# Attention forward and backward: six of eight blocks of E transposed on TensorE instead of seven, and the fp32 transposes of X spread over four steps

## The chip, the cores and the metric

One core of one Trainium2 chip runs the whole program in one launch. The metric is the device time in microseconds of one execution; a kernel's time is the median of several runs. A core has five engines with queues of their own: TensorE (PE; its weight loads are shown as PEld), VectorE (DVE), ScalarE (ACT), GpSimd (POOL) and SyncE (SP), which here only issues DMAs. Results of TensorE land in PSUM, in banks of 2 KB a partition; the DMA engines move data between DRAM and SBUF and can transpose blocks of 128 x 128 bf16 on the way. Engines wait for each other by semaphores.

## The reference

The kernel computes the output of a gated attention block and the gradients of all its inputs and weights. With 2048 tokens, width 512 and 32 heads of 16 columns:

```python
def _A_ref(x, wqkv, wo):
    qkv = (x @ wqkv).reshape(B, S, 3, H, Dh).transpose(2, 0, 3, 1, 4)
    q, k, v = qkv[0], qkv[1], qkv[2]
    p = softmax(einsum("bhqd,bhkd->bhqk", q, k) * Dh ** -0.5)
    o = einsum("bhqk,bhkd->bhqd", p, v)
    return o.transpose(0, 2, 1, 3).reshape(B, S, D) @ wo

def _B_ref(x, w1, b1, w2, b2):
    return gelu(layernorm(x) @ w1 + b1) @ w2 + b2

def _fwd_reference(...):
    xn = layernorm(x)
    return x + _A_ref(xn, wqkv, wo) * silu(_B_ref(xn, w1, b1, w2, b2))

_out, _vjp = jax.vjp(_f, A_x, A_wqkv, A_wo, B_w1, B_b1, B_w2, B_b2)
return (_out, *_vjp(grad_out))
```

## The kernel before

The program has three stages. The first computes projections and the gate and leaves operands for attention in DRAM. The second, `attention_core`, is the one that is changed; it lies between about 222 and 1882 us of the span. The third makes the gradients of the weights and of x.

Attention works on pairs of heads (`p`, 16 of them) and chunks of 512 queries (`qc`, four a pair), which makes 64 *blocks*. A block has 16 *steps*, one for each chunk of 128 keys, so the loop runs through 1024 steps `g` and then 20 more that only drain. Scores stand with keys on the partitions. One step handles both heads of the pair (`hj`), so it has an E (the exponentials of the scores) of 128 keys x 2 heads x 512 queries, and a G (E times the gradient that comes in, less a row term) of the same size.

The order within a step is written out by hand at the end of `attention_core`, and each engine runs its part in this order:

- TensorE multiplies out `d` of head 0 for step g (L1105), the scores `s` of both heads for step g+1 (L1083), and `d` of head 1. `s` has one PSUM buffer, `d` three.
- ACT makes E of step g+1 with one exponential (L1092), into a slot of the ring `ets`, which has three slots of four steps each.
- TensorE transposes E of step g-1 (L1167). E has eight blocks of 128 x 128 in a step: four groups of queries x two heads. Seven are transposed here, into the one PSUM buffer `tT`; the eighth is left to the DMA. Which block is left out alternates with every group of four steps, so that the blocks left out of two neighbouring groups lie side by side in `ets`.
- TensorE adds E and G of step g-1, times values and keys, to X (L1197, L1200, L1204), a sum over the block in one PSUM buffer. Then it does a share of Z, the gradients of keys and values (L1281), for the step 20 steps back, from transposed E (`ek`, `ekd`) and transposed G (`gk`).
- VectorE makes G as two products `gts`, one for each head (L1122). Between the two it copies up to two of the seven transposed blocks of step g-1 from `tT` to `ek` (L1179); the table `VCOPY` says how many in which step. After the last step of a block it copies X to SBUF as `xs` (L1213). Two times a block it adds Z to `acc` (L1293, L1295).
- ACT copies the rest of `tT` to `ek` (L1179).
- SyncE issues DMA transposes: in every odd step the two steps' G as a whole (`gk`, L1138, 16 blocks), and every eight steps the blocks of E that were left out (`ekd`): in one DMA of eight blocks where the two groups' slots are neighbours (L1154), otherwise in two of four (L1148, L1152).

In the third step of a block (`FIN_AT = 2`, counted from 0) the X of the block before is finished: TensorE transposes `xs` in four fp32 transposes into `XT`, one of the three buffers of `d` (L1223), VectorE copies it to `xt` (L1235) and takes a reciprocal (L1245), and GpSimd makes the weights W for Z, the attention output and the gradient of the queries.

Of the kernel before, what the change touches and what calls it, by code (L numbers as in the profile page):

```python
# [8 lines left out]
bf16 = mybir.dt.bfloat16  # L9
f32 = mybir.dt.float32  # L10
ACT = mybir.ActivationFunctionType
ALU = mybir.AluOpType
# [1006 lines left out]
def attention_core(ctx, ctx_r, tc, k, grads, Oall, dQall, dKVT_out, ident_f32, ident_bf, npairs=16, nqc=4):  # L1019
# [35 lines left out]
    NB = len(blocks)  # L1055
    NSTEP = NB * 16
    st_s, st_d, st_et, st_gt, st_T = {}, {}, {}, {}, {}
    blk = [dict(Gk={}, Ek={}) for _ in range(NB)]
    cur = {}

    def a_unit(g):
        return (g // 16, g % 16) if 0 <= g < NSTEP else None
# [43 lines left out]
                         start=True, stop=True, tile_position=(r, 0))  # L1106


    VCOPY = (0, 0, 0, 0, 1, 1, 1, 2, 1, 2, 0, 0, 1, 1, 1, 0)

    def emit_mult(g):
        a = a_unit(g)
        if a is None:
            emit_cT(g - 1, 7 - VCOPY[(g - 1) % 16], 7, nc.vector.tensor_copy)
            return
        kb = a[1]
        if kb % 2 == 0:
            cur["gts"] = gtp.tile([128, 2, 2, 512], bf16, name="gts")
        gts = cur["gts"]
        st_gt[g] = gts  # L1120
        for hj in range(2):
            nc.vector.tensor_tensor(out=gts[:, kb % 2, hj, :].rearrange("k (b q) -> k b q", b=4),  # L1122
                                    in0=st_d.pop((g, hj))[:].rearrange("k (b q) -> k b q", b=4),
                                    in1=st_et[g][:, :, hj, kb % 4, :], op=ALU.mult)
            if hj == 0:
                emit_cT(g - 1, 7 - VCOPY[(g - 1) % 16], 7, nc.vector.tensor_copy)

    def emit_dmat(g):
        a = a_unit(g)
        if a is None:  # L1130
            return
        j, kb = a
        kc = kb // 4
        if kb % 4 == 1:
            blk[j]["Gk"][kc] = gbp.tile([128, 4, 2, 4, 128], bf16, name="gk")
        if kb % 2 == 1:
            gk = blk[j]["Gk"][kc][:, kb % 4 - 1:kb % 4 + 1]
            nc.sync.dma_start_transpose(out=gk.rearrange("q r h b k -> q (r h b) k"), in_=st_gt[g][:].rearrange("k a h q -> k (a h q)"))  # L1138


        sl = g // 4 % 3
        if kb % 8 == 4:
            ek = ekd.tile([128, 2, 4, 128], bf16, name="ekd")
            blk[j]["Ek"][(kc - 1, 3)] = ek[:, 0]
            blk[j]["Ek"][(kc, 3)] = ek[:, 1]
            blk[j]["ekd"] = ek
            if sl == 0:
                nc.sync.dma_start_transpose(out=ek[:, 0], in_=ets[:, 2, 3, 1].rearrange("k a q -> k (a q)"))  # L1148
        if kb % 8 == 6:
            ek = blk[j].pop("ekd")  # L1150
            if sl == 0:
                nc.sync.dma_start_transpose(out=ek[:, 1], in_=ets[:, sl, 0, 0].rearrange("k a q -> k (a q)"))  # L1152
            else:
                nc.sync.dma_start_transpose(out=ek[:].rearrange("q c a k -> q (c a) k"),  # L1154
                                            in_=ets[:].rearrange("k s b h a q -> k (s b h) (a q)")[:, 8 * sl - 1:8 * sl + 1]
                                            .rearrange("k x q -> k (x q)"))

    def emit_T(g):
        a = a_unit(g)
        if a is None:  # L1160
            return
        kk = a[1] % 4
        et = st_et[g]
        t = ps_t.tile([128, 7, 128], bf16, name="tT")
        for i in range(7):
            b = i + a[1] // 4 % 2
            nc.tensor.transpose(t[:, i, :], et[:, b // 2, b % 2, kk, :], ident_bf[:])  # L1167
        st_T[g] = t
        if kk == 0:
            cur["ek"] = ekc.tile([128, 4, 7, 128], bf16, name="ek")  # L1170
            blk[a[0]]["Ek"][a[1] // 4] = cur["ek"]

    def emit_cT(g, lo, hi, copy):

        a = a_unit(g)
        if a is None or lo == hi:
            return
        j, kb = a
        copy(out=blk[j]["Ek"][kb // 4][:, kb % 4, lo:hi].rearrange("q i k -> q (i k)").bitcast(f32),  # L1179
             in_=st_T[g][:, lo:hi].rearrange("q i k -> q (i k)").bitcast(f32))  # L1180

    def emit_x(g, part):
        a = a_unit(g)
# [23 lines left out]
    def emit_xs(g):  # L1207
        a = a_unit(g)
        if a is None or a[1] != 15:
            return  # L1210
        j = a[0]
        xs = xsp.tile([128, 512], f32, name="xs", tag="xs")
        nc.vector.tensor_copy(out=xs[:], in_=blk[j].pop("X")[:])  # L1213
        blk[j]["xs"] = xs

    def emit_XT(g):
        j = g // 16 - 1
        if g % 16 != FIN_AT or not 0 <= j < NB:
            return
        xs = blk[j].pop("xs")  # L1220
        XT = ps_d.tile([128, 4, 128], f32, name="XT", tag="d")
        for qb in range(4):
            nc.tensor.transpose(XT[:, qb, :], xs[:, qb * 128:(qb + 1) * 128], ident_f32[:])  # L1223
        blk[j]["XT"] = XT

    def emit_fin(g):
        j = g // 16 - 1
        if g % 16 != FIN_AT or not 0 <= j < NB:
            return
        p, qc = blocks[j]  # L1230
        NQq = k.op0["NATQq"]
        NQd = k.op0["NATQd"]
        XT = blk[j].pop("XT")
        xt = xsp.tile([128, 4, 128], f32, name="xt", tag="xs")
        nc.vector.tensor_copy(out=xt[:], in_=XT[:])  # L1235
        xf = xt[:].rearrange("q b c -> q (b c)")
        XE = xf[:, 0:256].rearrange("q (b h c) -> q b h c", b=4, h=2)
        XG = xf[:, 256:512].rearrange("q (b h c) -> q b h c", b=4, h=2)
        W1, W2 = WT[j % 2]
        st0 = qc * 4  # L1240
        nqs = NQq[:, st0:st0 + 4, :, :]
        ndo = NQd[:, st0:st0 + 4, :, :]
        bc = lambda ap: ap.to_broadcast([128, 4, 2, 16])
        rL = finp.tile([128, 4, 2, 1], f32, name="rL")
        nc.vector.reciprocal(out=rL[:], in_=XG[:, :, :, 17:18])  # L1245
        nc.gpsimd.tensor_tensor(out=W2[:, :, :, 16:32], in0=nqs, in1=bc(rL[:]), op=ALU.mult)  # L1246
        ndl = finp.tile([128, 4, 2, 1], f32, name="ndl")
        nc.gpsimd.tensor_tensor(out=ndl[:], in0=XG[:, :, :, 0:1], in1=rL[:], op=ALU.mult)
        ndr = finp.tile([128, 4, 2, 1], f32, name="ndr")
        nc.gpsimd.tensor_tensor(out=ndr[:], in0=ndl[:], in1=rL[:], op=ALU.mult)  # L1250
        nc.gpsimd.tensor_tensor(out=W1[:, :, :, 0:16], in0=ndo, in1=bc(rL[:]), op=ALU.mult)
        nc.gpsimd.tensor_tensor(out=W1[:, :, :, 16:32], in0=nqs, in1=bc(ndr[:]), op=ALU.mult)
        Ov = Oall[:, st0:st0 + 4, p * 32:(p + 1) * 32].rearrange("q b (h c) -> q b h c", h=2)
        nc.gpsimd.tensor_tensor(out=Ov, in0=XE[:, :, :, 16:32], in1=bc(rL[:]), op=ALU.mult)
        t1 = finp.tile([128, 4, 2, 16], f32, name="t1")
        nc.gpsimd.tensor_tensor(out=t1[:], in0=XE[:, :, :, 0:16], in1=bc(ndl[:]), op=ALU.mult)
        nc.gpsimd.tensor_tensor(out=t1[:], in0=XG[:, :, :, 1:17], in1=t1[:], op=ALU.add)
        rL4 = finp.tile([128, 4, 2, 1], f32, name="rL4")
        nc.gpsimd.tensor_scalar(out=rL4[:], in0=rL[:], scalar1=0.25, scalar2=None, op0=ALU.mult)
        dQv = dQall[:, st0:st0 + 4, p * 32:(p + 1) * 32].rearrange("q b (h c) -> q b h c", h=2)  # L1260
        nc.gpsimd.tensor_tensor(out=dQv, in0=t1[:], in1=bc(rL4[:]), op=ALU.mult)

    def emit_z(g):
        u = z_unit(g)
        if u is None:
            return
        j, kp, qb, part = u
        if part == 0 and qb == 0:
            blk[j]["Z"] = ps_z.tile([128, 512], f32, name="Z", tag="z")
        Z = blk[j]["Z"]  # L1270
        for par in range(2):
            kc = 2 * kp + par
            for hj in range(2):
                r = 64 * par + 32 * hj
                if part == 0:
                    mv = blk[j]["Gk"][kc][:, :, hj, qb, :]
                elif 2 * qb + hj == 7 * (1 - par):
                    mv = blk[j]["Ek"][(kc, 3)]
                else:
                    mv = blk[j]["Ek"][kc][:, :, 2 * qb + hj - par, :]  # L1280
                nc.tensor.matmul(Z[r:r + 32, :], lhsT=WT[j % 2][1 - part][:, qb, hj, :], rhs=mv,  # L1281
                                 start=(part == 0 and qb == 0), stop=(part == 1 and qb == 3), tile_position=(0, r))

# [17 lines left out]
            for b in range(2):  # L1301
                nc.gpsimd.dma_start(out=dv[:, kp, b, :], in_=ob[b * 64:(b + 1) * 64, :])

    FIN_AT = 2
    ZOFF = -20
    late = []
    for hj in range(2):
# [2 lines left out]
    for g in range(NSTEP - ZOFF):  # L1310
# [32 lines left out]
        emit_acc(g + ZOFF)  # L1343
        if g >= NSTEP:
            grads.tail_mid(g - NSTEP)
        emit_cT(g - 1, 0, 7 - VCOPY[(g - 1) % 16], nc.scalar.copy)
        st_T.pop(g - 1, None)
        emit_dmat(g)
        st_gt.pop(g - 2, None)
# [117 lines left out]
```

## Time and profile before

| | us |
|---|---|
| runs before (three) | 2231.56, 2234.59, 2238.38; median 2234.59 |
| profiled execution, its own time | 2229.55 |
| its span, first to last instruction | 2227.8 |
| attention, 222 to 1882 us of the span: TensorE busy | 1640.0 of 1660 |
| VectorE busy there | 1548.7 |
| ScalarE busy there | 1448.6 |
| GpSimd busy there | 423.3 |
| mean granted TensorE clock | 0.993 |

The groups of instructions of the attention loop, as the profile gives them (line, engine, operation, out<-in, shapes, count | busy us, mean ns of one | idle us of the engine just before them and what ended most of it):

```profile
L1122 DVE TENSOR_TENSOR gts<-d,ets 128x512 bf16<-128x512 f32 x2048 | 1363.0, 684 | 99.5 <-ACT ek L1179 20.3
L1092 ACT ACTIVATE ets<-s 128x1024 bf16<-128x1024 f32 x1024 | 1048.7, 1024 | 196.9 <-PE s L1083 94.6
L1167 PE MATMUL tT<-ident_bf,ets 128*128 128x128 bf16 x7168 | 569.2, 219 | 15.9 <-ACT ek L1179 6.1
L1179 ACT COPY ek<-tT 128x448 f32<-128x448 f32 (+2 forms) x1024 | 501.6, 490 | 7.3 <-DVE ek L1179 6.1
L1179 DVE COPY ek<-tT 128x64 f32<-128x64 f32 (+1 forms) x576 | 132.4, 230 | 4.8 <-DMA DSO_s<-gd 3.5
```

A matmul record runs until its last result is out, and the next begins long before: seven transposes of 219 ns each start within half a microsecond. Sums of means of TensorE are therefore more than the time they take. One block of 128 x 128 bf16 is 64 fp32 columns wide in the copies of `tT`, so 448 columns are seven blocks. In all, `q1`, the queue of SyncE's DMAs, moves 424.67 MB; over the attention the DMA engines move 199 GB/s.

### The profile page before, as it was taken

To read this page: it belongs to the slowest core of one execution; us is meant where nothing else is said; L and a number is where in the kernel's file an instruction comes from. 1 tells how busy PE (TensorE), PEld (TensorE's weight loads), DVE (VectorE), ACT (ScalarE), POOL (GpSimd) and SP (SyncE) were. 2 spreads that over 40 slices of the span, in tenths; PEclk is the share of its full clock that TensorE was granted. 3 is DMA by queue.
4 is the path that set the end of the run, shared out by engine and by line. 5 is a ranking of instruction groups with operands and counts; after the bars stand their busy time and mean duration, and the time that the engine had idled before them with its cause. 6 is when DMAs were issued, how large, how long until landed. Compare 5 with 4: busy or idle time off the path is not lost.

```text
span 2227.8 us, 74213 instructions
## 1 busy us (share of the span) xinstructions
PE 2158.9 (97%) x30690; PEld 1204.8 (54%) x30690; DVE 1912.6 (86%) x3626; ACT 1734.3 (78%) x2481; POOL 607.5 (27%) x1387
## 2 busy tenths in 40 slices
PE   6999899999999999999999999999999999899998
PEld 3444455555555555555555555555555555344444
DVE  6676799999999999999999999999999998698624
ACT  5664888888888888888888888888888886584214
POOL 4276413222222222222312222222213223310002
PEclk9999999999999999999999999999999999999999
DMA  7785999999999999999999999999999999899874
GB/s 230 245 275 197 190 200 192 199 203 194 202 201 196 201 192 210 196 204 196 202 201 198 200 194 204 197 195 204 199 201 200 196 213 230 233 251 252 231 202 155
DMA packets 1421747, 461.15 MB, mean 207 GB/s; under 512 B 1334622, under 2 KB 1405662, under 8 KB 1421408
## 3 DMA queue, kind: packets, MB, share of 16 engines
q1 hardware_dynamic: 1406880, 424.67, 100.3%
q0 software_dynamic: 12944, 30.16, 5.2%
q8 instruction: 240, 3.93, 0.8%
q10 hardware_dynamic: 1584, 1.57, 0.2%
q14 instruction: 99, 0.81, 0.1%
HBM read 62.79 MB, written 64.75 MB: 57 GB/s over the span
## 4 chain that ended last, share of the span: by engine, by line
PE 89%; DVE 3%; DMA 3%; ACT 3%; issue 2%; SPq 1%; POOL 1%; DVEq 0%; ACTq 0%; POOLq 0%
PE tT L1167 24%; PE d L1105 14%; PE X L1197 10%; PE Z L1281 10%; PE X L1200 5%; PE X L1204 5%; PE s L1083 2%; PE ps_dw L729 2%; PE ps_dy L902 2%; PE ps_m L367 2%; PE ps_h L352 2%; PE ps_dw L974 2%; PE ps_dh L868 2%; PE XT L1223 1%; PE ps_qkv L210 1%
## 5 line engine op out<-in xcount | busy, mean ns | idle before, releaser
L1122 DVE TENSOR_TENSOR gts<-d,ets 128x512 bf16<-128x512 f32 x2048 | 1363.0, 684 | 99.5 <-ACT ek L1179 20.3
L1092 ACT ACTIVATE ets<-s 128x1024 bf16<-128x1024 f32 x1024 | 1048.7, 1024 | 196.9 <-PE s L1083 94.6
L1167 PE MATMUL tT<-ident_bf,ets 128*128 128x128 bf16 x7168 | 569.2, 219 | 15.9 <-ACT ek L1179 6.1
L1167 PEld LDWEIGHTS <-ets 128*128 128x128 bf16 x7168 | 445.7, 97 | 241.2 <-issue 239.3
L1179 ACT COPY ek<-tT 128x448 f32<-128x448 f32 (+2 forms) x1024 | 501.6, 490 | 7.3 <-DVE ek L1179 6.1
L1105 PE MATMUL d<-QDT,KVT 32*128 32x512 bf16 x2048 | 457.4, 385 | 0.0
L1083 PE MATMUL s<-QDT,KVT 32*128 32x512 bf16 x2048 | 401.3, 380 | 3.0 <-ACT ets L1092 2.7
L1105 PEld LDWEIGHTS <-KVT 32*128 32x128 bf16 x2048 | 145.2, 91 | 323.7 <-issue 323.7
L1197 PE MATMUL X<-ets,NAT 128*32 128x256 bf16 x4096 | 300.5, 284 | 0.1
L1204 PE MATMUL X<-gts,NAT 128*17 128x256 bf16 x4096 | 289.8, 273 | 0.0
L1200 PE MATMUL X<-ets,Lc 128*32 128x256 bf16 x4096 | 289.8, 273 | 0.0
L1341 POOL COPY tick<-gts 1x2 bf16<-1x2 bf16 x205 | 36.1, 176 | 604.5 <-DVE gts L1122 604.5
L1281 PE MATMUL Z<-gk,W 128*32 128x512 bf16 x2048 | 197.8, 379 | 1.0 <-DVE acc L1295 1.0
L1281 PE MATMUL Z<-ek,W 128*32 128x512 bf16 x1792 | 198.6, 379 | 0.0
L1246 POOL TENSOR_TENSOR W<-NATQq,rL 128x128 bf16<-128x128 bf16 x64 | 25.4, 397 | 525.2 <-DVE rL L1245 442.5
L1197 PEld LDWEIGHTS <-NAT 128*32 128x32 bf16 x4096 | 106.1, 93 | 110.9 <-issue 11.6
L1083 PEld LDWEIGHTS <-KVT 32*128 32x128 bf16 x2048 | 138.8, 91 | 11.2 <-issue 8.6
L1179 DVE COPY ek<-tT 128x64 f32<-128x64 f32 (+1 forms) x576 | 132.4, 230 | 4.8 <-DMA DSO_s<-gd 3.5
L1281 PEld LDWEIGHTS <-W 128*32 128x32 bf16 x4096 | 109.7, 97 | 11.5 <-issue 1.5
L1200 PEld LDWEIGHTS <-Lc 128*32 128x32 bf16 x4096 | 107.9, 96 | 0.0
L1204 PEld LDWEIGHTS <-NAT 128*17 128x17 bf16 x4096 | 103.5, 92 | 3.1
L1281 PE MATMUL Z<-ekd,W 128*32 128x512 bf16 x256 | 97.0, 379 | 0.0
(244 smaller groups left out, 2340.9 us busy)
## 6 DMA issues: line engine op xcount, KB each, us to landing
gk<-gts SPq DMA_TRANSPOSE x512, 5.2
H1T_s<-h1r SPq DMA_DIRECT2D x28, 256.0 KB, 4.0
HGT_s<-hgT SPq DMA_DIRECT2D x8, 896.0 KB, 4.5
DH_s<-stg SPq DMA_DIRECT2D x12, 512.0 KB, 3.4
hch<-DH_s SPq DMA_DIRECT2D x12, 512.0 KB, 4.4
gp<-H1T_s SPq DMA_DIRECT2D x9, 512.0 KB, 5.5
out_dram<-ob_w POOLq DMA_DIRECT2D x36, 128.0 KB, 4.3
NAT_s<-NS SPq DMA_DIRECT2D x4, 1056.0 KB, 6.1
```

The lines of the kernel that those rows point to most:

```text
L352: nc.tensor.matmul(ps[:], lhsT=w1_sb[:, ic, fc * 128:(fc + 1) * 128], rhs=yT[:, ic, g * 512:(g + 1) * 512], start=(ic == 0), stop=(ic == I ...
L367: nc.tensor.matmul(ps[:], lhsT=hgT[:, g % 2, fc, t4 * 128:(t4 + 1) * 128], rhs=w2_sb[:, fc, :], start=(fc == 0), stop=(fc == FC - 1))
L1083: nc.tensor.matmul(s[:, hj, :], lhsT=op["KVT"][r:r + 32, kb * 128:(kb + 1) * 128], rhs=op["QDT"][r:r + 32, qc * 512:(qc + 1) * 512], start ...
L1092: nc.scalar.activation(out=st_et[g][:, :, :, a[1] % 4, :].rearrange("k b h q -> k h b q"), in_=cur["s"][:].rearrange("k h (b q) -> k h b q ...
L1105: nc.tensor.matmul(d[:], lhsT=op["KVT"][r:r + 32, kb * 128:(kb + 1) * 128], rhs=op["QDT"][r:r + 32, qc * 512:(qc + 1) * 512], start=True, ...
L1122: nc.vector.tensor_tensor(out=gts[:, kb % 2, hj, :].rearrange("k (b q) -> k b q", b=4), in0=st_d.pop((g, hj))[:].rearrange("k (b q) -> k b ...
L1167: nc.tensor.transpose(t[:, i, :], et[:, b // 2, b % 2, kk, :], ident_bf[:])
L1179: copy(out=blk[j]["Ek"][kb // 4][:, kb % 4, lo:hi].rearrange("q i k -> q (i k)").bitcast(f32), in_=st_T[g][:, lo:hi].rearrange("q i k -> q ...
L1197: nc.tensor.matmul(X[r:r + 32, 0:256], lhsT=NATt[:, kb, hj, 1:33], rhs=ev, start=(kb == 0), stop=False, skip_group_check=True, tile_positi ...
L1200: nc.tensor.matmul(X[r:r + 32, 256:512], lhsT=Lc[:], rhs=ev, start=False, stop=False, skip_group_check=True, tile_position=(0, r))
L1204: nc.tensor.matmul(X[r:r + 17, 256:512], lhsT=NATt[:, kb, hj, 0:17], rhs=gv, start=False, stop=(kb == 15), skip_group_check=True, tile_pos ...
L1281: nc.tensor.matmul(Z[r:r + 32, :], lhsT=WT[j % 2][1 - part][:, qb, hj, :], rhs=mv, start=(part == 0 and qb == 0), stop=(part == 1 and qb = ...
```

## The change

- TensorE transposes six blocks of E in a step instead of seven; two blocks (both heads of one group of queries, the first or the last) are left to the DMA. The `ekd` DMA moves 16 blocks at once where it moved eight, and eight where it moved four, at the same places of the order. The tiles `ek` get smaller and `ekd` larger.
- The table `VCOPY` and VectorE's copies of `tT` go; ACT copies all six blocks (384 columns) in every step.
- `tT` becomes a whole PSUM bank. Its last 128 fp32 columns take one piece of X: in each of the steps 1 to 4 of a block one fp32 transpose stands behind the six of E, and VectorE copies its result, 128 columns, back into `xs`, between the two products of the step. The buffer of `d` that `XT` took is no longer used for it.
- VectorE copies X to `xs` in two halves. The reciprocal and the weights W follow the second piece, the output and the gradient of the queries the fourth.

```diff
 def emit_mult(g):
-                emit_cT(g - 1, 7 - VCOPY[(g - 1) % 16], 7, nc.vector.tensor_copy)
+                emit_xt(g)
...
 def emit_dmat(g):
+        fl = ets[:].rearrange("k s b h a q -> k (s b h) (a q)")
         if kb % 8 == 4:
-            ek = ekd.tile([128, 2, 4, 128], bf16, name="ekd")
+            ek = ekd.tile([128, 4, 4, 128], bf16, name="ekd")
...
             else:
                 nc.sync.dma_start_transpose(out=ek[:].rearrange("q c a k -> q (c a) k"),
-                                            in_=ets[:].rearrange("k s b h a q -> k (s b h) (a q)")[:, 8 * sl - 1:8 * sl + 1]
-                                            .rearrange("k x q -> k (x q)"))
+                                            in_=fl[:, 8 * sl - 2:8 * sl + 2].rearrange("k x q -> k (x q)"))
...
 def emit_T(g):
-        t = ps_t.tile([128, 7, 128], bf16, name="tT")
-        for i in range(7):
-            b = i + a[1] // 4 % 2
-            nc.tensor.transpose(t[:, i, :], et[:, b // 2, b % 2, kk, :], ident_bf[:])
+        t = ps_t.tile([128, 512], f32, name="tT")
+        tb = t[:].bitcast(bf16).rearrange("q (i k) -> q i k", k=128)
+        for i in range(6):
+            b = i + 2 * (a[1] // 4 % 2)
+            nc.tensor.transpose(tb[:, i, :], et[:, b // 2, b % 2, kk, :], ident_bf[:])
...
-    def emit_cT(g, lo, hi, copy):
+    def emit_cT(g):
...
+        nc.scalar.copy(out=blk[j]["Ek"][kb // 4][:, kb % 4].rearrange("q i k -> q (i k)").bitcast(f32), in_=st_T[g][:, 0:384])
...
 def emit_xs(g):
-        nc.vector.tensor_copy(out=xs[:], in_=blk[j].pop("X")[:])
+        X = blk[j].pop("X")
+        for h in (1, 0):
+            nc.vector.tensor_copy(out=xs[:, 256 * h:256 * h + 256], in_=X[:, 256 * h:256 * h + 256])
...
+    def fin_part(g):
+        j = g // 16 - 1
+        i = g % 16 - FIN_AT
+        return (j, (2, 3, 0, 1)[i]) if 0 <= j < NB and 0 <= i < 4 else None
...
 def emit_XT(g):
-        XT = ps_d.tile([128, 4, 128], f32, name="XT", tag="d")
-        for qb in range(4):
-            nc.tensor.transpose(XT[:, qb, :], xs[:, qb * 128:(qb + 1) * 128], ident_f32[:])
+        t = st_T[g - 1] if a_unit(g - 1) is not None else ps_d.tile([128, 512], f32, name="XT", tag="d")
+        nc.tensor.transpose(t[:, 384:512], blk[j]["xs"][:, i * 128:(i + 1) * 128], ident_f32[:])
...
+    def emit_xt(g):
...
+        nc.vector.tensor_copy(out=blk[j]["xs"][:, i * 128:(i + 1) * 128], in_=blk[j].pop("XT"))
...
-    FIN_AT = 2
+    FIN_AT = 1
```

## The prediction

> **What bounds the kernel now.** I read the page first. TensorE looks like the bound: 97% busy. The page says itself that a busy PE isn't PE at its peak, so I went on to the timeline of a few attention steps, because one step repeats 1024 times.
>
> ```profile
> PE 2158.9 (97%) x30690; PEld 1204.8 (54%) x30690; DVE 1912.6 (86%) x3626; ACT 1734.3 (78%) x2481; POOL 607.5 (27%) x1387
> ...
> L1083 PE MATMUL s<-QDT,KVT x2048: 371/384/604, 222.1 to 1868.2; 32*128 32x512 bf16 x187
> ```
>
> The second line is the view of the score matmuls by source line: first to last start, 1646.1 us for 1023 steps, so 1.609 us a step.
>
> ```profile
> 1202.37 1.02 ACT L1092 ACTIVATE ets<-s 128x1024 bf16<-128x1024 f32 x1 [0.17 <-PE s L1083]
> ...
> 1202.93 0.21 DVE L1179 COPY ek<-tT 128x64 f32<-128x64 f32 x1
> ...
> 1203.29 0.47 ACT L1179 COPY ek<-tT 128x384 f32<-128x384 f32 x1
> ...
> 1203.44 0.39 PE L1083 MATMUL s<-QDT,KVT 32*128 32x512 bf16 x2
> ...
> 1203.81 0.55 PE L1167 MATMUL tT<-ident_bf,ets 128*128 128x128 bf16 x7
> ...
> 1203.93 1.02 ACT L1092 ACTIVATE ets<-s 128x1024 bf16<-128x1024 f32 x1 [0.17 <-PE d L1105]
> ```
>
> In this timeline (start, duration) the exponential ends at 1203.39; `s`, which has one buffer, is overwritten from 1203.44; its matmuls end at 1203.83; the next exponential starts at 1203.93. That ring is 1.02 + 0.05 + 0.39 + 0.10 = 1.56 us and holds no transpose. A second wait ends in step: the ACT copy ends at 1203.76 and the next transposes, into the one `tT` buffer, start at 1203.81. TensorE's own round is shorter. It shows right after a block's end, where TensorE is late and waits for nobody:
>
> ```profile
> 1206.58 0.39 PE L1105 MATMUL d<-QDT,KVT 32*128 32x512 bf16 x1
> ...
> 1206.99 0.55 PE L1167 MATMUL tT<-ident_bf,ets 128*128 128x128 bf16 x7
> ...
> 1207.91 0.29 PE L1197 MATMUL X<-ets,NAT 128*32 128x256 bf16 x4
> ...
> 1208.58 0.38 PE L1105 MATMUL d<-QDT,KVT 32*128 32x512 bf16 x1
> ...
> 1210.06 0.38 PE L1105 MATMUL d<-QDT,KVT 32*128 32x512 bf16 x1
> ```
>
> `d` to `d` is 1.48 from 1208.58 (no wait) and 2.00 from 1206.58 (the step with four fp32 transposes of X). So ring 1.56 against round 1.48: the ring of ACT and `s` is the bound, and TensorE's high share is mostly pipelined records and waiting. 1024 x 1.56 = 1597; the loop takes 1024 x 1.609 = 1648. **Some 50 us is all that anything but a shorter ring can win.**
>
> **The change, part by part.**
>
> *One bf16 transpose fewer a step.* Seven span 0.55 with 0.219 for one, so the pitch is (0.55 - 0.219)/6 = 0.055: 1024 x 0.055 = 56 us off TensorE's order. The round falls to 1.43, but the ring stays 1.56. I take 0; the cover is the ring, and without it this would be worth up to the 50 us above.
>
> *VectorE's copies of `tT` go (132.4 us busy); ACT always copies 384 (0.47) in place of 320, 384 or 448 (0.42 to 0.53).* Exponential and copy overlap by 0.10, so ACT needs 0.92 + 0.47 of 1.56, and in the steps with 448 the copy's 0.05 delays the transposes to just when the ring is due: 0.53 - 0.10 + 0.05 + 1.14 (transposes to next `d`, 1202.25 to 1203.39 in the timeline) = 1.62 after the exponential's end, against 1.61 for `s`. Worth 0 to 0.01 a step: 0.
>
> *X's fp32 transposes spread over four steps.* Four cost 1207.91 - 1206.99 - 0.48 = 0.44, 0.11 each. Over the four steps 1 to 4 of a block, `s` starts at 1205.01, 1206.59, 1208.58, 1210.16, 1211.73: 6.72 for 6.24, so 0.48 a block or 31 us over 64 blocks. In the changed step the round is 1.43 + 0.11 = 1.54 < 1.56: hidden, gain up to 31 us.
>
> *What takes their place.* The transposed piece now lies in the bank of `tT`. In the built program ACT's copy of `tT` waits in these four steps for VectorE's copy of X's piece, which stands behind the first `gts` product of its step; behind ACT's copy stand the next exponential and the next transposes. The trace of before has this pattern where VectorE took a column of `tT`: 1202.93 + 0.21, then ACT at 1203.29. Two `gts` are late: after the copy of X (L1213) in step 0, and after the accumulation (L1293) in step 3.
>
> ```profile
> 1205.19 0.68 DVE L1213 COPY xs<-X 128x512 f32<-128x512 f32 x1
> ...
> 1206.41 0.53 ACT L1179 COPY ek<-tT 128x448 f32<-128x448 f32 x1
> ```
>
> By forms, 64 columns take 215 ns, 128 281, 512 681, so 256 some 414; the two halves take 0.75 with their overlap of 0.08, 0.07 more than now. The product behind them then runs 1205.86 to 1206.54, the 128-column copy ends at 1206.74, ACT's copy starts at 1206.79 in place of 1206.41: 0.38 late. It ends at 1207.26, the transposes start at 1207.31, and `d` follows 1.14 - 0.055 + 0.11 = 1.195 later at 1208.50, against 1208.15 due by the ring: 0.35 lost. The same sum in step 4 gives ACT 0.23 late, of which 0.11 is lost. Steps 2 and 3 close a ring of six transposes and X's 0.70, copy 0.33, ACT's copy 0.52, wait 0.05 = 1.60: 0.04 each. Together 0.54 a block for 0.48: **+4 us**. Bounds: nothing late at all, -31; each lateness paid in full, 0.38 + 0.23 + 0.08 = 0.69, +13.
>
> The Trainium skill, PSUM — Partial Sum Buffer, "PSUM bank collisions raise a hardware error", says that two engines must be kept apart on one bank, reads against reads too. The trace agrees in that ACT's copy waited for VectorE's (6.1 us, 10 times, in the list of waits). If the rule weren't needed, this item would be -31 and not +4.
>
> *Two of eight blocks by DMA.* In 85 places one transfer of 8 blocks (L1154) becomes one of 16, as large as a `gk`; the other 43 pairs go from 4 to 8 blocks and have time. It frees the slot of `ets` that the exponential five steps on overwrites, so behind a late one stands the ring itself. SyncE issues it between two `gk`.
>
> ```profile
> L1138 SPq DMA_TRANSPOSE gk<-gts x512: 1587/2241/4588, 228.5 to 1872.8; - x171
> ...
> DMA to landing us min/median/max: 3.6/5.2/8.8
> ...
> L1154 SPq DMA_TRANSPOSE ekd<-ets x85: 1261/1267/2529, 239.9 to 1857.8; - x85
> ...
>   ACT ets L1092: 4.7, 7
> ...
> DMA to landing us min/median/max: 2.4/3.5/5.9
> ```
>
> These are the views of the tiles `gk` and `ekd` (ns least/median/most of an issue; landings, for `ekd` of the 4-block ones). 3.5 us for 4 blocks, 5.2 for 16: 8 more blocks cost (5.2 - 3.5) x 8/12 = 1.1 us. The exponential already waited 7 times. Following the 85 transfers to their exponentials in the trace, the landing comes a median 1.3 us ahead, and under 0.8 in a quarter of them. Pushing all 85 by 1.1 us makes about 36 late, by 21 us in all; by 1.5, 60 late and 41 us. SyncE issues 4 x 2.24 + 1.27 = 10.2 us in 8 steps (12.9) now and 5 x 2.24 = 11.2 of 12.5 then, so queues get longer; each stall gives the queue time back. I take **+28 us**, between the two pushes' 21 and 41 for the fuller queue. Bounds: 0 if the landings stay as they are (more blocks can't land sooner, so not below), 105 if the queue itself sets the pace (rivals).
>
> By the Trainium skill, Advanced Engine Details and Errata, "X-Bar Transpose (TRN2)", transposes move at 350 to 400 GB/s: an estimate of 0.7 us for the 256 KB more, and some 10 us late in place of 28. The trace is slower: 199 GB/s over the attention.
>
> **Sum.** The profiled execution took 2229.55 (span 2227.8). 2229.55 + 0 + 4 + 28 = 2261.6. The median of the runs, 2234.59, is 5.0 above it: **2266.6**.
>
> **Rivals.** *Faster.* The ring alone sets every step: the spread transposes hide and the DMAs land in time. -31 on the median gives 2204; if the whole 50 us goes, 2185. For it: round 1.54 under ring 1.56, VectorE loses 132 us of copies. Against: the late products, the margins. It decides if ACT's copies in steps 1 and 4 wait under 0.1 us and the 16-block transfers land within about 5.5 us of issue. *They cancel.* The spread wins its 31 and lateness costs 28: 2232. *The queue becomes the bound.* If SyncE's issues go to 2.74 us, the median that the `gk` of step 7 of a block, right behind an `ekd`, have now, 8 steps need 13.7 us, 1.71 each: +0.10 x 1024 = 105 us, 2340. For it: 90% of SyncE's time is booked; against: an unhindered issue takes 1.59.
>
> **Chances.** Mine, slower by a ring that waits for bank and DMA: 0.50, own range 2242 to 2320. Faster 0.24. Cancel 0.12. Queue 0.14. Less than 0.3% (7 us) is no change for this measurement. So faster 0.24, same 0.12, slower 0.64. The range 2212 to 2320 leaves out the best of the faster case and most of the queue's.
>
> **What would show it.** Right: steps in a block's middle still 1.56 with `s` 0.05 behind the exponential; no step of 2.00 but late ACT copies behind X's small copies in steps 1 and 4; tens of waits of `ets` on `ekd`, some 30 us; landings of `ekd` of 5 us or more. Wrong: a step under 1.56 as a rule (then the ring wasn't the bound), or waits on `ekd` under 10 us.

## The result, and the profile after

The changed kernel takes 2307.36 us (median of four runs, 2297.73 to 2311.57) against 2236.48 for the kernel before (four runs, 2231.56 to 2238.38). The ratio is 1.0314 with an interval of 1.0276 to 1.0353: 71 us slower. The forecast was 32 us slower (2266.6 against 2234.59). The profiled execution took 2309.86 us, its span is 2308.1.

First the page's line of busy times, then the view of the score matmuls by source line (least/median/most ns, first and last start), both of the changed kernel:

```profile
PE 2172.8 (94%) x29666; PEld 1166.5 (51%) x29666; DVE 1843.9 (80%) x3306; ACT 1726.2 (75%) x2481; POOL 609.3 (26%) x1387
```

```profile
L1083 PE MATMUL s<-QDT,KVT x2048: 371/384/605, 222.1 to 1946.4; 32*128 32x512 bf16 x187
```

All three big shares fell, TensorE's from 97% to 94%: the engines wait more (VectorE also has less to do). The loop runs from 222.1 to 1946.4, 1.6855 us a step for 1.609. That is 78 us more over 1023 steps, and the two profiled executions lie 80 us apart, so nearly the whole loss lies in the loop.

The groups of the loop, as the page of the changed kernel gives them, answer to those of before (idle time of the engine just before them, and what ended most of it, stand last):

```profile
L1120 DVE TENSOR_TENSOR gts<-d,ets 128x512 bf16<-128x512 f32 x2048 | 1327.4, 684 | 246.7 <-PE d L1105 108.2
L1092 ACT ACTIVATE ets<-s 128x1024 bf16<-128x1024 f32 x1024 | 1048.0, 1023 | 254.7 <-PE d L1105 121.7
L1166 PE MATMUL tT<-ident_bf,ets 128*128 128x128 bf16 x6144 | 517.4, 221 | 31.6 <-ACT ek L1177 31.3
...
L1177 ACT COPY ek<-tT 128x384 f32<-128x384 f32 x1024 | 486.0, 475 | 35.1 <-DVE xs L1234 25.3
```

Three things are new. VectorE, rid of its 132 us of copies, stands idle 247 us ahead of its products instead of 100. ACT's copy of `tT` waits 25.3 us for VectorE's small copy of X's piece (L1234). The exponential waits 254.7 for 196.9. What it waits for is in the list of waits (us in total, times, longest):

```profile
ACT ets L1092 <- DMA ekd<-ets: 64.1, 40, 4.6
PE s L1083 <- ACT ets L1092: 50.8, 38, 4.1
```

It is the DMA that must free the slot of `ets`: 64.1 us in 40 places for 4.7 us in 7. The second line is the same stalls handed on, since `s` can't be overwritten before the exponential has read it. The views of the two tiles that the DMA transposes show the transfers themselves, first `gk`, then `ekd` (its landings are those of the 8-block transfers):

```profile
L1136 SPq DMA_TRANSPOSE gk<-gts x512: 1583/2242/7076, 228.5 to 1951.5; - x171
...
DMA to landing us min/median/max: 3.6/5.3/9.1
```

```profile
L1153 SPq DMA_TRANSPOSE ekd<-ets x85: 1660/2397/4260, 240.8 to 1936.2; - x85
...
DMA to landing us min/median/max: 2.8/4.2/8.3
```

The median `gk` is what it was; the longest issue went from 4.6 to 7.1 us. The typical step has not changed either. In the timeline of the changed kernel (start, duration), in the middle of a block:

```profile
1101.32 1.02 ACT L1092 ACTIVATE ets<-s 128x1024 bf16<-128x1024 f32 x1 [0.17 <-PE d L1105]
...
1102.24 0.47 ACT L1177 COPY ek<-tT 128x384 f32<-128x384 f32 x1
...
1102.40 0.39 PE L1083 MATMUL s<-QDT,KVT 32*128 32x512 bf16 x2
...
1102.89 1.02 ACT L1092 ACTIVATE ets<-s 128x1024 bf16<-128x1024 f32 x1 [0.17 <-PE d L1105]
```

The exponentials are 1.57 apart and `s` starts 0.06 behind one's end: the ring of 1.56 that the prediction named. The 78 us aren't spread over the steps. Following the trace step by step, 20 steps in which TensorE stands idle for over 1 us hold 49 us above 1.60 a step; 39 steps close behind such stalls, at a granted clock under 0.95, hold another 20; the other 964 average 1.619.

### The profile page after: what moved, and what is told of

It is laid out like the page before. It is cut to its first block, busy times and chain, and to the rows that moved or that the text cites. A ratio compares the mean times of both kernels' runs of the same rounds, so it can differ in the third digit from the quotient of the medians.

```text
span 2308.1 us, 71753 instructions
## 1 busy us (share of the span) xinstructions
PE 2172.8 (94%) x29666; PEld 1166.5 (51%) x29666; DVE 1843.9 (80%) x3306; ACT 1726.2 (75%) x2481; POOL 609.3 (26%) x1387
## 3 DMA queue, kind: packets, MB, share of 16 engines
q10 hardware_dynamic: 1584, 1.57, 0.2%
## 4 chain that ended last, share of the span: by engine, by line
PE 71%; DMA 11%; DVE 9%; ACT 5%; issue 2%; POOL 1%; SPq 1%; DVEq 0%; ACTq 0%; POOLq 0%
PE tT L1166 16%; PE d L1105 10%; DMA ekd<-ets 9%; PE X L1194 8%; PE Z L1294 7%; DVE gts L1120 5%; PE s L1083 4%; PE X L1197 4%; PE X L1201 4%; PE ps_dw L729 2%; PE ps_dy L902 2%; PE ps_m L367 2%; PE ps_h L352 2%; ACT ets L1092 2%; PE ps_dw L974 2%
## 5 line engine op out<-in xcount | busy, mean ns | idle before, releaser
L1120 DVE TENSOR_TENSOR gts<-d,ets 128x512 bf16<-128x512 f32 x2048 | 1327.4, 684 | 246.7 <-PE d L1105 108.2
L1092 ACT ACTIVATE ets<-s 128x1024 bf16<-128x1024 f32 x1024 | 1048.0, 1023 | 254.7 <-PE d L1105 121.7
L1166 PE MATMUL tT<-ident_bf,ets 128*128 128x128 bf16 x6144 | 517.4, 221 | 31.6 <-ACT ek L1177 31.3
L1166 PEld LDWEIGHTS <-ets 128*128 128x128 bf16 x6144 | 381.9, 98 | 271.7 <-issue 269.8
L1177 ACT COPY ek<-tT 128x384 f32<-128x384 f32 x1024 | 486.0, 475 | 35.1 <-DVE xs L1234 25.3
L1105 PE MATMUL d<-QDT,KVT 32*128 32x512 bf16 x2048 | 511.0, 390 | 1.3 <-DVE gts L1120 1.3
L1083 PE MATMUL s<-QDT,KVT 32*128 32x512 bf16 x2048 | 406.3, 385 | 51.0 <-ACT ets L1092 50.8
L1105 PEld LDWEIGHTS <-KVT 32*128 32x128 bf16 x2048 | 163.0, 91 | 330.4 <-issue 330.4
L1294 PE MATMUL Z<-gk,W 128*32 128x512 bf16 x2048 | 203.3, 390 | 1.0 <-DVE acc L1308 1.0
L1083 PEld LDWEIGHTS <-KVT 32*128 32x128 bf16 x2048 | 160.8, 91 | 84.0 <-issue 68.0
L1255 POOL TENSOR_TENSOR W<-NATQq,rL 128x128 bf16<-128x128 bf16 x64 | 25.3, 396 | 530.7 <-DVE rL L1254 446.8
L1234 DVE COPY xs<-tT 128x128 f32<-128x128 f32 x252 | 71.2, 283 | 6.4 <-PE tT L1226 5.0
```

The costliest lines, as they stand in the source:

```text
L1083: nc.tensor.matmul(s[:, hj, :], lhsT=op["KVT"][r:r + 32, kb * 128:(kb + 1) * 128], rhs=op["QDT"][r:r + 32, qc * 512:(qc + 1) * 512], start ...
L1092: nc.scalar.activation(out=st_et[g][:, :, :, a[1] % 4, :].rearrange("k b h q -> k h b q"), in_=cur["s"][:].rearrange("k h (b q) -> k h b q ...
L1105: nc.tensor.matmul(d[:], lhsT=op["KVT"][r:r + 32, kb * 128:(kb + 1) * 128], rhs=op["QDT"][r:r + 32, qc * 512:(qc + 1) * 512], start=True, ...
L1166: nc.tensor.transpose(tb[:, i, :], et[:, b // 2, b % 2, kk, :], ident_bf[:])
L1177: nc.scalar.copy(out=blk[j]["Ek"][kb // 4][:, kb % 4].rearrange("q i k -> q (i k)").bitcast(f32), in_=st_T[g][:, 0:384])
L1234: nc.vector.tensor_copy(out=blk[j]["xs"][:, i * 128:(i + 1) * 128], in_=blk[j].pop("XT"))
```

## The experiments

Two theories for the DMA term. By the *deadline* theory (the prediction's) only the 85 transfers of 16 blocks are late, because the exponential five steps on needs them; take the hurry away and the loss goes. By the *queue* theory the transposes as a whole no longer fit beside the loads and the rest, and whatever is queued costs its own length, wherever the wait then shows. For the spread of X: the two late products cost, or they are hidden.

All diffs are against the changed kernel, unless they say otherwise.

### One block by DMA instead of two, one transpose fewer all the same

```diff
-            ek = ekd.tile([128, 4, 4, 128], bf16, name="ekd")
+            ek = ekd.tile([128, 2, 4, 128], bf16, name="ekd")
...
-                                            in_=fl[:, 8 * sl - 2:8 * sl + 2].rearrange("k x q -> k (x q)"))
+                                            in_=fl[:, 8 * sl - 1:8 * sl + 1].rearrange("k x q -> k (x q)"))
...
-                    mv = blk[j]["Eo"][kc][:, hj]
+                    mv = blk[j]["Eo"][kc][:, 0]
```

> The changed kernel with the DMA moving one block of E a step, as before, instead of two; Z reads the block of head 0 for both heads, so one block of the eight is left out. Deadline theory (the 16-block transfer lands after the exponential wants its slot of ets; that is some 60 of the 71 us): 2240 to 2255 us, waits of ets on ekd under 10 us. Queue theory (SyncE and the DMA engines have too many bytes): the same 2240 to 2255. Bank theory (the cost is ACT waiting for VectorE on the bank of tT): 2290 us or more.

2234.0 us against 2233.76, ratio 1.0003 (0.999 to 1.0016). The exponential's waits for `ekd` are 10.9 us. So the second block in the queue costs 2307 - 2234 = 73 us, all of the loss, and the rest of the change together is worth nothing. Both theories had expected this, though at least 6 us more.

### The same with X finished as before, and the change with X finished as before

The functions that finish X are those of the kernel before; the first of the two kernels has the edit above as well.

```diff
-        for h in (1, 0):
-            nc.vector.tensor_copy(out=xs[:, 256 * h:256 * h + 256], in_=X[:, 256 * h:256 * h + 256])
+        nc.vector.tensor_copy(out=xs[:], in_=blk[j].pop("X")[:])
...
-        nc.tensor.transpose(t[:, 384:512], blk[j]["xs"][:, i * 128:(i + 1) * 128], ident_f32[:])
+        XT = ps_d.tile([128, 4, 128], f32, name="XT", tag="d")
+        for qb in range(4):
+            nc.tensor.transpose(XT[:, qb, :], xs[:, qb * 128:(qb + 1) * 128], ident_f32[:])
...
-    FIN_AT = 1
+    FIN_AT = 2
```

> The changed kernel with one block of E a step by DMA (Z reads the block of head 0 for both heads, one of eight left out) and X finished as before, four fp32 transposes at once. Against the same with X spread (2234 us): if the spread wins what the four at once cost and pays it back on the bank of tT (0.54 for 0.48 us a block), 2230 us; if the spread is a gain that the late DMAs hid, 2250 to 2265 us; if the bank costs more than the spread wins, 2215 to 2227 us.

2212.25 us, 0.9911 (0.989 to 0.9932). The step is (1845.9 - 221.3)/1023 = 1.588.

> The changed kernel with X finished as before: four fp32 transposes at once in step 2 of a block, in a buffer of d, one copy of 512 columns. Deadline and queue theory: the new way of X costs some 10 us, so 2290 to 2305 us, waits on ekd still some 60 us. Bank theory: 2235 to 2250 us.

2301.82 us, 1.0319 (1.028 to 1.0358).

With one block in the queue, the spread of X costs 2234 - 2212 = 22 us; with two, 5. Read the other way round, the second block costs 73 us with X spread and 2302 - 2212 = 90 with X finished as before: the prices depend on the order in which they are taken. "The rest is worth nothing" was a sum of two terms that cancel: -21 and +22. Where the queue sets the pace, most of what the loop wins or loses elsewhere doesn't show.

### Six transposes in the kernel before, and all copies by ACT in it

Against the kernel before; the first leaves the seventh block out, the second changes one table.

```diff
-        for i in range(7):
+        for i in range(6):
...
-                    mv = blk[j]["Ek"][kc][:, :, 2 * qb + hj - par, :]
+                    mv = blk[j]["Ek"][kc][:, :, min(5, 2 * qb + hj - par), :]
```

> The kernel before with six transposes of E a step in place of seven, and nothing else taking the seventh: its block is left out and Z reads another in its place; the copies get one block narrower. If the ring of exponential and s is the bound (1.56 us): 2225 to 2240 us, steps still 1.56. If TensorE is the bound: 1024 x 0.055 = 56 us less, 2180 us.

2222.43 us, 0.9948 (0.9932 to 0.9964): -11, for the transpose and the one block less that is copied.

```diff
-    VCOPY = (0, 0, 0, 0, 1, 1, 1, 2, 1, 2, 0, 0, 1, 1, 1, 0)
+    VCOPY = (0,) * 16
```

> The kernel before, complete, with ACT copying all seven blocks of tT in every step (VCOPY all 0). By the sum of the prediction the wider copy delays the transposes to just when the ring is due: 2230 to 2240 us. If VectorE's share was the better one for the late steps: 2245 us or more.

2237.12 us, 1.0014 (1.0004 to 1.0025): +4. So VectorE's copies were worth keeping with seven blocks, if only just, where ACT would copy 448 columns each time, and the -21 needs both parts of the change at once: the transpose gone (-11) and, with only six to copy, VectorE's copies gone (-10, the difference between 2212 and 2222, with whatever else sets those two kernels apart).

### The pieces of X in other steps

```diff
-        i = g % 16 - FIN_AT
-        return (j, (2, 3, 0, 1)[i]) if 0 <= j < NB and 0 <= i < 4 else None
+        i = {2: 2, 3: 3, 5: 0, 6: 1}.get(g % 16)
+        return (j, i) if 0 <= j < NB and i is not None else None
```

> The changed kernel with one block of E a step by DMA (one of eight left out, as in e1) and the pieces of X in steps 2, 3, 5 and 6 of a block in place of 1 to 4, so that none stands behind a product that the copy of X or the accumulation made late. If those two late products are what the spread costs: 2205 to 2218 us. If ACT waits on the bank wherever a piece stands: 2230 us or more.

On top of the first experiment: 2207.81 us, 0.9886 (0.9868 to 0.9905), 26 under it. Steps 1 and 4 of a block were the ones where the first product is late, behind the copy of X and behind `acc`; now no piece lies there. The timeline of the first experiment shows what the 26 us were (the copies and products on VectorE, ACT's copy, the next transposes and scores):

```profile
1023.06 0.74 DVE L1212 COPY xs<-X 128x256 f32<-128x256 f32 x2
...
1023.72 0.68 DVE L1120 TENSOR_TENSOR gts<-d,ets 128x512 bf16<-128x512 f32 x1
...
1024.32 0.28 DVE L1234 COPY xs<-tT 128x128 f32<-128x128 f32 x1
...
1024.52 0.39 PE L1083 MATMUL s<-QDT,KVT 32*128 32x512 bf16 x2
1024.63 0.48 ACT L1177 COPY ek<-tT 128x384 f32<-128x384 f32 x1 [0.22 <-DVE xs L1234]
...
1025.16 0.49 PE L1166 MATMUL tT<-ident_bf,ets 128*128 128x128 bf16 x6 [0.25 <-ACT ek L1177]
...
1026.36 0.39 PE L1083 MATMUL s<-QDT,KVT 32*128 32x512 bf16 x2
...
1028.25 0.68 DVE L1308 TENSOR_TENSOR acc<-Z,acc 128x512 f32<-128x512 f32 x1
...
1029.76 0.48 ACT L1177 COPY ek<-tT 128x384 f32<-128x384 f32 x1 [0.30 <-DVE xs L1234]
```

Read it as a chain: X's copy, the product behind it, X's small copy, then ACT's copy (0.22 idle), then the transposes (0.25 idle), and `s` comes 1.84 us after the last one instead of 1.56. It happens again behind `acc`, with 0.30. In the lists of waits ACT's copy waits 26.2 us in 100 places for the small copies there, and 0.2 us in one place with the pieces moved. The two copies read different columns of one bank and touch no common word. That agrees with the rule that the prediction cited (the Trainium skill, PSUM — Partial Sum Buffer, "PSUM bank collisions raise a hardware error"). The wait stands in the built program; no run leaves it out, so whether the chip needs it isn't shown.

> The changed kernel, complete, with only the pieces of X moved to steps 2, 3, 5 and 6. With one block by DMA this won 26 us against steps 1 to 4. If the DMA stalls are paid on top of that: 2278 to 2288 us. If the queue sets the pace so that what the steps win is lost in later landings: 2295 to 2307 us.

The same edit in the complete changed kernel: 2298.44 us, 1.0292 (1.0263 to 1.032). Of the 26 us, 9 are left.

Against the kernel before, X's transposes in two pairs, in steps 2 and 6 of a block, in a buffer of `d`:

```diff
-        if g % 16 != FIN_AT or not 0 <= j < NB:
+        if g % 16 not in (2, 6) or not 0 <= j < NB:
...
-        XT = ps_d.tile([128, 4, 128], f32, name="XT", tag="d")
-        for qb in range(4):
+        XT = ps_d.tile([128, 2, 128], f32, name="XT", tag="d")
+        q0 = 2 if g % 16 == 2 else 0
+        for qb in range(2):
```

> The kernel before, complete, with X finished in two pairs of fp32 transposes, in steps 2 and 6, each in a buffer of d. A pair costs 0.22 us against 0.08 us that TensorE has in a step and gets back in the next: 2220 to 2230 us. If taking a buffer of d twice makes d wait for VectorE: 2234 us or more.

2240.9 us, 1.0038 (1.0021 to 1.0055), 7 slower. Spreading X's transposes in this way isn't a gain while seven bf16 transposes stand beside them. A part of the loss is the second buffer: `d` now waits 10.0 us in 48 places for VectorE's products to free one, which it didn't before.

### The hurry taken out: two transfers of eight blocks, the urgent one two steps sooner

```diff
+            lo = (8 * sl - 2) % 24
+            nc.sync.dma_start_transpose(out=ek[:, 0:2].rearrange("q c a k -> q (c a) k"), in_=fl[:, lo:lo + 2].rearrange("k x q -> k (x q)"))
...
+            nc.sync.dma_start_transpose(out=ek[:, 2:4].rearrange("q c a k -> q (c a) k"), in_=fl[:, 8 * sl:8 * sl + 2].rearrange("k x q -> k (x q)"))
```

> The changed kernel with the same blocks by DMA, but always as two transfers of eight: the one of the slot that is overwritten first is issued two steps sooner. Deadline theory: 2245 to 2265 us, waits of ets on ekd under 15 us. Queue theory: bytes and issues are no fewer, so 2295 us or more. Bank theory: 2295 us or more.

2302.64 us, 1.0306 (1.0288 to 1.0323). This run, together with the moved loads further below, decides between the theories. From the list of waits of this kernel:

```profile
DVE gts L1120 <- DMA gk<-gts: 80.7, 75, 3.7
```

and from the view of the tile `ekd`, who waited for it:

```profile
  ACT ets L1092: 0.8, 3
```

The wait that the prediction had priced is gone, 0.8 us in 3 places, and the time is the same within 5 us. In its place VectorE's products wait 80.7 us in 75 places for a free `gts` buffer, which `gk` transfers hold. These were 4.7 us in 4 places in the changed kernel. The deadline theory falls: the wait only showed who came first to a full queue. One doubt is left by this run alone, since it issues 85 transfers more. But two issues of eight blocks take 1.26 us each where one of 16 took 2.40, so SyncE has hardly more to do.

### More in the queue, and less

Three blocks by DMA, five on TensorE:

```diff
-        for i in range(6):
-            b = i + 2 * (a[1] // 4 % 2)
+        for i in range(5):
+            b = i + 3 * (a[1] // 4 % 2)
...
-                                            in_=fl[:, 8 * sl - 2:8 * sl + 2].rearrange("k x q -> k (x q)"))
+                                            in_=fl[:, 8 * sl - 3:8 * sl + 3].rearrange("k x q -> k (x q)"))
```

> The changed kernel one step further: TensorE transposes five of eight blocks, the DMA three; 24 blocks in the transfer that had 16. Queue theory (at ten blocks a step the DMA queue is full, 1.66 us a step or 0.166 us a block): 11 x 0.166 = 1.83 us a step, 2440 to 2500 us. Deadline theory (each late transfer costs what it lands later, 0.8 to 1.1 us for 85 transfers): 2375 to 2400 us.

2414.24 us, 1.0821 (1.0791 to 1.0851): another 107 us, which lies between the two expectations and meets neither. The step is (2063.4 - 221.4)/1023 = 1.8006 in the profiled execution, 0.115 above the changed kernel's; this execution took 2425.67 and was the slowest of the four, and by the medians it is 107/1024 = 0.104.

The operand loads of GpSimd taken out (only the first loads of the loop are left):

```diff
-                L = natq_loads(k, k.op0, p, nc.gpsimd.dma_start) if p > 0 else []
-                if p + 1 < npairs:
+                L = []
+                if p == 0:
```

> The changed kernel without the loads of operands that GpSimd issues during attention: only the first two pairs' operands are loaded and all pairs use them, so the result of attention is that of two pairs. Queue theory with the loads as the disturbance (a transfer of transposes stands while some of the 16 engines serve DRAM packets): 2240 to 2275 us. If the transposes alone fill the queue: 2295 us or more.

2234.24 us, 1.0007 (0.9994 to 1.0019): -73, as much as the second block cost, though not one transpose was taken away. (It is 6 us under what was expected.) SyncE issues the same transposes as before, so it isn't its issuing by itself that was full. GpSimd's queue of DMAs, from the changed kernel and from this one (packets, MB, share):

```profile
q0 software_dynamic: 12944, 30.16, 4.7%
```

```profile
q0 software_dynamic: 5904, 14.97, 2.2%
```

That is 15.2 MB less, and 73 us for them are 208 GB/s.

> Three of eight blocks by DMA, without GpSimd's loads of operands (the first two pairs' serve all). If the DMA's parts add up, with 0.105 us a block and step (107 us from ten blocks to eleven) and at least 73 us for the loads: 2310 to 2345 us. If loads hinder in a way of their own, apart from the time that is booked: 2235 to 2260 us.

The edits of the last two runs together: 2343.21 us, 1.0501 (1.0471 to 1.0531), 71 under the run with three blocks.

> The changed kernel without GpSimd's loads of operands (the first two pairs' operands serve all pairs) and with the pieces of X in steps 2, 3, 5 and 6. If without the loads the DMA queue has room for ten blocks even at a shorter step: 2204 to 2216 us, as with one block by DMA. If the queue sets the pace there too: 2225 to 2236 us.

No loads, two blocks, and the pieces of X in steps 2, 3, 5 and 6: 2221.47 us, 0.9947 (0.9932 to 0.9962), which is 14 above the kernel with one block and those steps.

With ten blocks a step in the queue (eight of G, two of E) the loads cost 73 us, with eleven 71; the eleventh block costs 107 with loads and 109 without. The terms add, as they do in a resource whose time has become the step's. Nine blocks with loads and ten without both take 2234, but not for the same reason. With nine the loop sets the time, since it fell by 26 us when the pieces of X were moved; with ten and no loads it fell by 13 only, so there the queue lies just beyond the loop's own time. Only what lies beyond is paid.

### The loads on another queue, and in other steps

Both kernels have the pieces of X in steps 2, 3, 5 and 6 as well.

```diff
-                    L += op_load_list(k, OP[(p + 1) % 2], p + 1, nc.gpsimd.dma_start)
+                    L += op_load_list(k, OP[(p + 1) % 2], p + 1, nc.sync.dma_start)
```

> The changed kernel, complete, with the pieces of X in steps 2, 3, 5 and 6 and the loads of operands issued by SyncE in the queue of the transposes instead of by GpSimd. If a load costs because its packets come between those of a transposing transfer on a second queue: 2205 to 2225 us, faster than both kernels. If a load takes the same time from the DMA engines on any queue: 2270 to 2295 us.

```diff
-                    late.append((g + 16 * (i // 4) + 6 + 3 * (i % 4), f))
+                    late.append((g + 16 * (i // 4) + (11, 12, 18, 19)[i % 4], f))
```

> The changed kernel, complete, with the pieces of X in steps 2, 3, 5 and 6 and GpSimd's loads moved from steps 6, 9, 12 and 15 of a block to steps 11, 12, 2 and 3, where the exponential that needs a slot of ets has just had it. If a load costs only where it falls into an ekd transfer that is awaited: 2225 to 2255 us. If it costs wherever it stands because the queue is full on average: 2275 to 2300 us.

They stand against 2298.44. Issued by SyncE the loads give 2316.47 (1.0363, 1.0327 to 1.0399), moved to other steps 2314.95 (1.0362, 1.0321 to 1.0403). Neither helps, both cost some 17 us, and both lie above either of their expectations. Why they cost anything stays open. The deadline theory would have had the moved loads at 2225 to 2255. And since the loads come no cheaper when SyncE issues them, it isn't GpSimd's part in a load that is dear.

> The kernel before with the loads of operands issued by SyncE. With nine blocks a step the queue has room and the waits on ekd are 4.7 us in all: 2226 to 2236 us. If loads in the transposes' own queue delay them more than on a second one: over 2240 us.

The loads issued by SyncE in the kernel before: 2234.71 us, 1.0005 (0.999 to 1.0019). With nine blocks it doesn't matter which engine issues the loads, since the queue has room.

No kernel that computes everything came under the kernel before.

## Why the prediction went wrong in size

By the runs the change is 2233 - 21 + 22 + 73 = 2307; the prediction had 0, +4 and +28. The direction was right, and 2307 lies in the range that was given. But the first two terms were both missed, and that they come to +1 where +4 was forecast is luck. The signs that were named for being right came up, the late ACT copies and tens of waits of `ets` on `ekd`; they show where a wait ends, not what it is worth.

*The bound.* Right. The ring of exponential and `s`, 1.56 us, sets the steps in a block's middle in both kernels. With X finished as before and one block by DMA, one step after another runs at 1.55, which is the same ring to a hundredth.

*One transpose fewer and VectorE's copies gone: 0 predicted, -21 measured* (2212 against 2233; -11 for the transpose alone). The ring covers most steps but not all. The prediction's own example had a step of 2.00 that was TensorE's, where four fp32 transposes stand beside seven others; with six beside them and X finished as before it is 1.89. The term should have been split by kind of step. The upper bound, 50, was sound.

*The spread of X: +4 predicted, +22 measured.* The mechanism was right in each link: the two late products, ACT's copy held up behind the small copy, the transposes behind ACT's copy, then `s`. ACT stood idle for 0.22 and 0.30; counted as the prediction counts, from where the copy would start 0.10 before the exponential's end, the copies came 0.32 and 0.40 late where 0.38 and 0.23 were worked out. Over the six steps of the timeline above `s` takes 10.07 us from 1022.91 to 1032.98 for 9.36 by the ring: 0.71 lost, where 0.54 had been worked out for four of them. What was off more was what it is held against: four fp32 transposes in one step cost 0.48 only while seven bf16 transposes stand beside them, and that slack had gone to the other term.

*Two blocks by DMA: +28 predicted, +73 measured. This is the step that failed.* The prediction followed the 85 transfers of 16 blocks to their exponentials, pushed each by the 1.1 us that eight more blocks take, and counted how much came late, with the words that "each stall gives the queue time back". In the changed kernel the exponentials did wait for `ekd`, 64.1 us in 40 places, where 36 late ones and 21 us had been worked out for the lower push. But a wait at one consumer is not a price. With that wait taken out the time stayed, and the wait came up at another consumer of the same queue. What was to be added was the queue's time a step, transposes and loads together, and held against the ring. Whatever lies above the loop's own time is paid: 73 us of the second block, the whole 107 to 109 of the third. The loads, which the prediction left out altogether, are 71 to 73 us of that time.

*The rival "the queue becomes the bound"* named this mechanism and gave it 0.14. Its price, 105, came from longer issues by SyncE; 73 was measured, and the median issue of a `gk` stayed at 2.24. The evidence for it was in the prediction, "90% of SyncE's time is booked", and was outweighed by a single unhindered issue of 1.59 us. A booked share of nine tenths on a queue that serves two buffers of two engines should have weighed more. *Faster*: its part in X was there, but in other steps than those of the change (2207.81 with one block in the queue). *They cancel*: this is what happened without the second block, 2234, by other terms.

## What to carry over

Treat a DMA queue that runs transposes as an engine: add up its time a step, loads on other queues included, and compare it with the loop's bound, before asking which transfer is due when. If moving the one transfer that is waited for doesn't change the time, look for the new wait at another consumer; the resource behind both is the bound. And place a small copy that shares a PSUM bank with a critical one in steps where nothing stands ahead of it on its engine.

## What the runs showed of the hardware

**Behind a stall the granted TensorE clock falls.** Windows of 1 us of the changed kernel (the sum column, then the busy times of PE, PEld, DVE, ACT and POOL, the granted TensorE clock, the DMA share and GB/s), around a wait of the exponential for `ekd`:

```profile
1029.00:1030.00 1.00, 0.89 (x17) 0.27 (x10) 1.00 (x4) 0.00 (x0) 0.92 (x4) 1.00 1.08 244
1030.00:1031.00 1.00, 0.00 (x0) 0.00 (x0) 0.53 (x1) 0.00 (x0) 0.12 (x1) 1.00 1.28 287
1031.00:1032.00 1.00, 0.00 (x0) 0.00 (x0) 0.00 (x0) 0.76 (x1) 0.00 (x0) 1.00 1.26 287
1032.00:1033.00 1.00, 0.69 (x9) 0.46 (x9) 0.65 (x1) 0.83 (x3) 0.00 (x0) 1.00 1.12 252
1033.00:1034.00 1.00, 1.00 (x21) 0.55 (x18) 0.71 (x3) 1.00 (x2) 0.30 (x1) 0.63 1.20 275
1034.00:1035.00 1.00, 1.00 (x13) 0.15 (x6) 0.22 (x1) 0.20 (x1) 0.92 (x4) 0.50 1.18 250
1035.00:1036.00 1.00, 1.00 (x18) 0.75 (x18) 0.87 (x2) 0.84 (x1) 0.59 (x2) 0.50 1.28 290
1036.00:1037.00 1.00, 1.00 (x20) 0.31 (x12) 0.42 (x1) 0.55 (x2) 0.00 (x0) 0.67 0.36 78
```

TensorE is idle for 2.42 us; soon after it starts again the granted clock falls to 0.50 and stays there for over 3 us, and the steps take over 2 us. Of the 20 stalls of over 1 us in the loop, 16 had such a stretch within 6 us of their end, the shortest of them 1.58 us long, while some of up to 2.19 went without. The Trainium skill, TensorE: Matmul & The Clock Gate, Part 1: The HAM clock gate (the "warmup" mystery), puts the fall to half clock after an idle window of about 3.4 us; here it fell behind idle times of less than half of that. The mean clock fell with the stalls: 0.993 before, 0.981 after, 0.957 with three blocks. How much of the 20 us in the slow steps is a cost of its own, on top of the 49 in the stalls, stays open. While TensorE is slow the queue catches up, and the run without the hurry has 7 us in such steps for 20, but is only 5 us faster by the medians (14 by the loops of the two profiles).

**The transposes stop for other packets.** Windows of half a microsecond of the changed kernel, the same columns (the DMA share counts all packets by their whole time, and they overlap, so it can exceed 1):

```profile
1312.50:1313.00 0.50, 0.50 (x19) 0.33 (x16) 0.50 (x2) 0.50 (x1) 0.34 (x1) 1.00 1.25 285
...
1314.00:1314.50 0.50, 0.50 (x20) 0.35 (x17) 0.50 (x2) 0.50 (x1) 0.00 (x0) 1.00 5.09 55
1314.50:1315.00 0.50, 0.50 (x16) 0.19 (x4) 0.50 (x1) 0.50 (x2) 0.00 (x0) 1.00 0.01 1
1315.00:1315.50 0.50, 0.50 (x9) 0.29 (x6) 0.22 (x1) 0.33 (x2) 0.00 (x0) 1.00 0.08 9
...
1317.00:1317.50 0.50, 0.50 (x18) 0.38 (x19) 0.50 (x2) 0.50 (x1) 0.36 (x1) 1.00 1.32 117
```

The queue runs at 285 GB/s in the first window and comes nearly to a stop for three. A packet of 16 KB of the instruction queue starts at 1314.01 and takes 0.96 us. Over the 159 such packets between 400 and 1700 us the transposing packets that start fall from 0.9 a ns to 0.1 for about 1 us. In the last window packets of a 128 KB load that GpSimd issued at 1312.24 are still on their way, and the rate is down to 117. From the first packets of a load the transposing packets that start fall from about 1.0 a ns to 0.3 to 0.7 for about 1 us if it has 64 KB, and to 0.1 to 0.25 for three quarters of one if it has 264 KB. That is how 13 loads a pair of heads can cost 71 to 73 us. They needn't cost more than their own bytes: the 208 GB/s that they come to is about the rate at which all DMAs of this loop move, below. No run separates the two. That the instruction packets cost their time too is read from the trace alone: they weren't taken away in any run. The 0.104 us that the eleventh block adds to a step by the medians, 32 KB, is a rate of 314 GB/s (285 by the two profiles). None of the windows shown goes above 290, so a part of the block's time may still be hidden. The estimate in the prediction from the Trainium skill, Advanced Engine Details and Errata, "X-Bar Transpose (TRN2)", went by 350 to 400; over five stretches of 300 us of the attention all DMAs of the changed kernel together move 207 to 212.
